# Cosine layer of a three-stage kernel: column slices in pairs, summed in one PSUM bank

## The chip, the cores and the metric

The kernel runs on one core of one Trainium2 chip. The metric is the device time of one execution in microseconds, the median of three runs. The engines are named as the profile names them: PE is TensorE (PEld its weight loads), DVE VectorE, ACT ScalarE, POOL GpSimd, SP SyncE.

## What is computed

The reference, cut to what matters here, chains an attention, a layer with a cosine in it, and a mixture of four ReLU experts over 2304 tokens of width 512:

```python
x = attn_out.transpose(0, 2, 1, 3).reshape(2304, 512)   # from 4 batches, 8 heads, 576 rows
# cosine layer: w_in 512 x 2048, w_out 2048 x 512
h = x @ w_in
g = h * np.cos(h)
x = g @ w_out
# experts: w1 4 x 512 x 1024, w2 4 x 1024 x 512
for e in range(4):
    out += p[:, e:e + 1] * (np.maximum(x @ w1[e], 0.0) @ w2[e])
```

The weights of the cosine layer come as 64-bit floats. The kernel narrows them to 32 bits itself, with integer operations.

## The kernel before

Every matrix product is done in split form: each operand is a high and a low part, and `mm3` issues three matmuls for one product.

Only the cosine layer changes. Its 2048 hidden columns are cut in 8 slices `s` of 256, its tokens in 4 batches `b` of 576. One (slice, batch) is a **unit**, and the list `order` (L410 and L411) holds 32 units, numbered `n`: first slices 0 and 1 batch by batch (n = 0 to 7), then each slice from 2 to 7 with its four batches (n = 8 to 31). A unit goes in two halves, `th` = 0 and 1, of 288 columns. For each half:

- `hidden1` (L353): 12 matmuls into `hp`, then a chain: ACT scales (`y`, L373) and rounds (`kk`, L375), DVE subtracts (L376), ACT takes the sine (L384), DVE multiplies (L385), ACT makes the high part of `gt` and POOL the low part (both L98 and L99 in `split`).
- `output1` (L389): 24 matmuls, 6 into each of four PSUM banks `op`, one for each 128 output rows `d`. DVE empties each bank: a copy for slice 0 (L404), an add into the accumulator `acc` in SBUF (L406) for the others. The output of a half is issued two halves after its hidden part (list `pend`).

Before its hidden part a unit needs `vw`, the slice's weights projected by the attention's small factor. In the later stage `project_two` (L333) does this for two units at once, 16 short matmuls each, on a 64x32 tile of the array.

A slice's weights come by `load_in` and `load_out`. Each calls `narrow` (L117) on two blocks; a block is one DMA, one ACT operation and three DVE operations (L127, L128, L131). `load_out` also splits the result (L104 on ACT, L106 shared between POOL and DVE). In `step1` the weights of slice s+1 are loaded during the four units of slice s: one block in each unit.

In time the kernel has three stages. Up to about 165 us the attention runs, eight parts of it, with the units n = 0 to 5 between them. Then, with `wide` set, hidden parts are worked in one piece of 576 columns and n = 6 to 31 follow without other work, up to about 456 us. The experts (L557 to L642) take the rest. At the seam `build_x` (L490, on DVE and ACT) prepares the experts' input, and `load2` (L523) loads and prepares their first two weight sets on the ACT queue, POOL, ACT and DVE, at marks taken from the last hidden parts. The weight sets lie in the pool `wc`, on the right side of SBUF where the attention's tiles were. A list scheduler fixes the order of instructions on each engine.

## Time and profile before

| | us |
|---|---|
| median of 3 runs | 1225.07 (1224.25 to 1225.99) |
| the profiled execution | 1226.03 |
| its span in the trace | 1223.9 |
| PE busy | 1178.7 (96% of the span) |
| DVE busy | 878.6 (72%) |
| POOL busy | 524.2 (43%) |
| ACT busy | 485.7 (40%) |

About 2.1 us of the profiled execution lie outside the span. A share of busy time is a mean over three unlike stages, so the table alone does not say what limits any one of them; the rows further down go stage by stage. A matmul's busy time overlaps its neighbour's, so for PE the distances between starts tell more than the busy time.

### The profile page before, as it was taken

Reading aid. Unit: us, or ns where it says so; the run is one execution under the profiler, and the core shown is the slowest. Engines: PE = TensorE matmul, PEld = TensorE weight load, DVE = VectorE, ACT = ScalarE, POOL = GpSimd, SP = SyncE. Lnnn points to the kernel's source line nnn. Section 1 sums busy time; section 2 is a strip of 40 time slices with the busy share of each in tenths; the row PEclk is TensorE's granted clock in tenths of the full one; section 3 lists DMA queues with packets and bytes.
Section 4 is the critical chain, followed back from the end, with each engine's and each line's share of the span. In section 5 each row is a group of like instructions: output and inputs, shape, how many; then the busy total and the mean of one; then the engine's idle time right before and its main releaser. Section 6 shows DMA issues by size and latency. Waiting matters only on the chain.

```text
span 1223.9 us, 20033 instructions
## 1 busy us (share of the span) xinstructions
PE 1178.7 (96%) x7946; PEld 1051.9 (86%) x7946; DVE 878.6 (72%) x1566; ACT 485.7 (40%) x854; POOL 524.2 (43%) x612
## 2 busy tenths in 40 slices
PE   7788999999999989999999999999999999999998
PEld 5566789999899888889899898888989889888997
DVE  5897988988888688666666666678666666666665
ACT  2475666666566663232223223244222322322221
POOL 0443533332333852445345444546544544453420
PEclk7598999999999999999999999999999999999999
DMA  9952011111112110111111111113211111111102
GB/s 223 249 155 71 21 35 53 52 39 62 39 53 70 37 51 18 35 52 53 35 52 53 35 36 54 50 36 118 63 35 42 60 38 35 53 52 36 52 1 78
DMA packets 50318, 72.88 MB, mean 60 GB/s; under 512 B 4913, under 2 KB 33585, under 8 KB 50225
## 3 DMA queue, kind: packets, MB, share of 16 engines
q1 hardware_dynamic: 43344, 55.88, 16.2%
q10 hardware_dynamic: 6880, 15.73, 4.2%
q8 instruction: 62, 1.02, 0.3%
q14 instruction: 32, 0.25, 0.1%
HBM read 66.88 MB, written 4.72 MB: 59 GB/s over the span
## 4 chain that ended last, share of the span: by engine, by line
PE 70%; DVE 16%; DMA 7%; ACT 3%; issue 2%; POOL 1%; SPq 0%; ACTq 0%; DVEq 0%; POOLq 0%
PE op L142 37%; PE hp L142 30%; DVE acc L406 3%; DVE y L376 2%; DMA raw<-in_moe_w_out_dram 2%; DMA raw<-in_moe_w_in_dram 2%; DVE y L385 2%; DVE raw L127 1%; DVE raw L128 1%; PE kvp L218 1%; DMA raw<-in_moe_w_dram 1%; DMA q<-in_q_dram 1%; DMA phi<-in_phi_dram 1%; DVE x L506 1%; DMA kv<-in_v_dram 1%
## 5 line engine op out<-in xcount | busy, mean ns | idle before, releaser
L142 PE MATMUL op<-wb,ht 128*128 128x512 f32 x1728 | 439.3, 396 | 0.0
L142 PEld LDWEIGHTS hp<-x,wa 128*128 128x128 f32 x2688 | 380.3, 189 | 24.5 <-DVE x L506 3.7
L142 PE MATMUL hp<-x,wa 128*128 128x320 f32 (+1 forms) x2688 | 393.5, 295 | 3.3 <-DVE x L506 3.0
L142 PEld LDWEIGHTS op<-wb,ht 128*128 128x128 f32 x1728 | 312.7, 188 | 58.4
L638 DVE SCALAR_TENSOR_TENSOR acc<-op,p_all,acc 128x512 f32<-128x512 f32 x270 | 201.6, 748 | 137.0 <-PE op L142 136.8
L142 PE MATMUL op<-gt,wo 128*128 128x288 f32 x1536 | 229.9, 300 | 12.3 <-DVE acc L406 5.3
L142 PEld LDWEIGHTS op<-gt,wo 128*128 128x128 f32 x1536 | 210.2, 189 | 26.8 <-DVE acc L406 7.5
L106 POOL TENSOR_TENSOR wb<-raw,wb 128x256 fp32r<-128x256 f32 x124 | 90.1, 757 | 224.4 <-ACT wb L104 224.4
L609 ACT ACTIVATE ht<-c 128x256 fp32r<-128x256 f32 (+3 forms) x128 | 71.8, 562 | 283.5 <-DVE c L579 283.5
L99 POOL TENSOR_TENSOR gt<-y,gt 128x576 fp32r<-128x576 f32 x52 | 81.1, 1559 | 159.0 <-ACT gt L98 108.7
L610 DVE SCALAR_TENSOR_TENSOR ht<-c,ht 128x256 fp32r<-128x256 f32 (+3 forms) x128 | 94.7, 740 | 63.1 <-ACT ht L609 63.1
L549 POOL TENSOR_TENSOR wa<-raw,wa 128x256 fp32r<-128x256 f32 x96 | 69.4, 749 | 148.5 <-ACT wa L539 148.5
L142 PE MATMUL hp<-attnT,vw 128*128 128x288 f32 x768 | 120.7, 304 | 7.3 <-DVE y L385 6.8
L142 PEld LDWEIGHTS hp<-attnT,vw 128*128 128x128 f32 x768 | 108.3, 192 | 14.1 <-issue 5.0
L579 DVE TENSOR_TENSOR c<-hp,u 128x256 f32<-128x256 f32 (+1 forms) x192 | 87.3, 457 | 42.3 <-PE hp L142 37.9
L549 POOL TENSOR_TENSOR wa<-tt,wa 128x256 fp32r<-128x256 f32 x128 | 110.7, 894 | 2.3 <-PE op L142 1.2
L406 DVE TENSOR_TENSOR acc<-op,acc 128x288 f32<-128x288 f32 x224 | 95.8, 448 | 9.1 <-PE op L142 9.0
L586 ACT COPY p<-hp 128x256 f32<-128x256 f32 x64 | 25.7, 401 | 112.5 <-PE hp L142 112.5
L384 ACT ACTIVATE y<-y 128x576 f32<-128x576 f32 (+1 forms) x76 | 46.1, 608 | 51.2 <-DVE y L376 42.2
L98 ACT ACTIVATE gt<-y 128x576 fp32r<-128x576 f32 (+1 forms) x76 | 46.1, 606 | 38.6 <-DVE y L385 38.5
L376 DVE SCALAR_TENSOR_TENSOR y<-kk,y 128x576 f32<-128x576 f32 x52 | 52.0, 1000 | 8.0 <-ACT kk L375 7.5
L385 DVE TENSOR_TENSOR y<-hp,y 128x576 f32<-128x576 f32 (+1 forms) x76 | 49.6, 653 | 7.6 <-ACT y L384 7.5
(101 smaller groups left out, 1035.0 us busy)
## 6 DMA issues: line engine op xcount, KB each, us to landing
raw<-in_moe_w_dram SPq DMA_DIRECT2D x60, 512.0 KB, 3.5
raw<-in_moe_w_out_dram ACTq DMA_DIRECT2D x14, 512.0 KB, 3.5
raw<-in_moe_w_in_dram ACTq DMA_DIRECT2D x12, 512.0 KB, 3.7
kv<-in_k_dram SPq DMA_DIRECT2D x16, 288.0 KB, 5.8
kv<-in_v_dram SPq DMA_DIRECT2D x16, 288.0 KB, 6.6
q<-in_q_dram SPq DMA_DIRECT2D x8, 576.0 KB, 8.2
out_dram<-acc SPq DMA_DIRECT2D x18, 256.0 KB, 2.0
phi<-in_phi_dram SPq DMA_DIRECT2D x8, 288.0 KB, 6.9
```

The lines of the kernel that those rows point to most:

```text
L98: nc.scalar.activation(out=hi, in_=src, func=ACTF.Copy)
L99: (eng or nc.vector).tensor_tensor(out=lo, in0=src, in1=f32(hi), op=ALU.subtract)
L106: (nc.vector if early and c % 512 else nc.gpsimd).tensor_tensor(out=t[:, 1, c:c + 256], in0=src[:, c:c + 256], in1=f32(t[:, 0, c:c + 256]) ...
L142: nc.tensor.matmul(out=ps, lhsT=lt(a), rhs=rt(b), start=first and i == 0, stop=last and i == 2, skip_group_check=more,)
L376: nc.vector.scalar_tensor_tensor(out=y, in0=kk, scalar=ROUND, in1=y, op0=ALU.subtract, op1=ALU.subtract)
L385: nc.vector.tensor_tensor(out=y, in0=hv, in1=y, op=ALU.mult)
L406: nc.vector.tensor_tensor(out=dst, in0=op[:, :TH], in1=dst, op=ALU.add)
L549: pool.tensor_tensor(out=wa[:, 1, o], in0=src, in1=f32(wa[:, 0, o]), op=ALU.subtract)
L579: nc.vector.tensor_tensor(out=out, in0=ps[:, :n], in1=sb, op=ALU.add)
L609: nc.scalar.activation(out=ht[:, 0, fc, lo:], in_=c[:, fc, lo:], func=ACTF.Relu)
L610: nc.vector.scalar_tensor_tensor(out=ht[:, 1, fc, lo:], in0=c[:, fc, lo:], scalar=0.0, in1=f32(ht[:, 0, fc, lo:]), op0=ALU.max, op1=ALU.su ...
L638: nc.vector.scalar_tensor_tensor(out=dst, in0=op, scalar=pe, in1=dst, op0=ALU.mult, op1=ALU.add)
```

## The change

The units of n = 2 to 7 and those of slices 3 to 6 are worked in **pairs** of slices with the same batch: hidden parts of both slices, then one output that sums the products of both slices in the same PSUM bank (12 matmuls to a bank) and empties the bank once. Slice 2 (n = 8 to 11) and slice 7 (n = 28 to 31) stay single, as do n = 0 and 1. The output of a pair goes to the queue in two entries of two banks each. `gt` gets a fourth buffer.

A pair needs the weights of two slices, so the loads move: both slices 3 and 4 are loaded during the four units of slice 2 (two blocks in a unit), slices 5 and 6 during n = 12 to 19 (one block in a unit), slice 7 during n = 20 to 23, none in n = 24 to 27. The tiles of slices 2, 5 and 6 lie in a new pool `wd` on the right side, where attention's were; `wc` opens after `wd` is closed.

```diff
-            wi[s] = cw.tile([128, KD, FS], F32, tag="wi", name="wi")
+            wi[s] = (wd[0] if s in (2, 5, 6) else cw).tile([128, KD, FS], F32, tag="wi", name="wi")
...
-        gt = cs.tile([128, 2, NFC, TH], F32R, tag="g", name="gt", bufs=3)
+        gt = cs.tile([128, 2, NFC, TH], F32R, tag="g", name="gt", bufs=4)
...
-    def output1(s, b, th, gt, wo):
-        for d in range(KD):
+    def output1(units, th, gts, ds):
+        b = units[0][1]
+        k = len(units)
+        for d in ds:
...
-            for fc in range(NFC):
-                mm3(
...
+            for j, (s, _) in enumerate(units):
+                for fc in range(NFC):
+                    mm3(
+                        op[:, :TH],
+                        lambda x: wo[s][:, x, fc, d * 128:d * 128 + 128],
+                        lambda x: gts[j][:, x, fc, :],
+                        j == 0 and fc == 0,
+                        j == k - 1 and fc == NFC - 1,
+                    )
...
-    order += [(s, b) for s in range(2, NS1) for b in range(B)]
...
+    order += [(2, b) for b in range(B)]
+    order += [(s, b) for s0 in (3, 5) for b in range(B) for s in (s0, s0 + 1)]
+    order += [(7, b) for b in range(B)]
+    assert NS1 == 8 and len(order) == NS1 * B
+    groups, n0 = [], 0
+    for n in [1, 1] + [2] * (B - 1) + [1] * B + [2] * (2 * B) + [1] * B:
+        groups.append(list(range(n0, n0 + n)))
+        n0 += n
+
+    jobs = {}
+    for j, n in enumerate((8, 9, 10, 11)):
+        for th in range(2):
+            jobs[n, th] = ((load_in, load_in, load_out, load_out)[j], (3, 4, 3, 4)[j], th)
+    for j in range(8):
+        jobs[12 + j, 0] = ((load_in, load_in, load_out, load_out)[j // 2], (5, 6, 5, 6)[j // 2], j % 2)
+    for j in range(4):
+        jobs[20 + j, 0] = ((load_in, load_out)[j // 2], 7, j % 2)
...
+    def layer1():
+        for gi, group in enumerate(groups):
+            pair = len(group) == 2
+            for th in range(2):
+                gts = []
+                for k, n in enumerate(group):
+                    if (n, th) in jobs:
+                        f, s, part = jobs[n, th]
+                        f(s, marks[-1], part)
+                    gts.append(hidden1(order[n][1], th, vws[n]))
+                    units = [order[i] for i in group]
+                    if not pair:
+                        queue.append((units, th, gts, range(KD)))
+                    elif k == 1:
+                        queue.extend((units, th, gts, ds) for ds in (range(0, 2), range(2, 4)))
+                    if len(queue) + (pair and k == 0) > 2:
+                        output1(*queue.pop(0))
+                    if (th, k) == (int(pair), 0):
+                        project_next(gi)
+                    yield
...
+    wd_ctx = ExitStack()
+    wd[0] = wd_ctx.enter_context(tc.tile_pool(name="wd", bufs=2, side="right", reuse_waits="tile"))
+    load_in(2)
+    next(steps)
+    next(steps)
+    load_out(2)
+    for _ in steps:
+        pass
+    for p in queue:
+        output1(*p)
+    wd_ctx.close()
     wc = ctx.enter_context(tc.tile_pool(name="wc", bufs=2, side="right", reuse_waits="tile"))
```

Over the whole program the adds of L406 fall from 224 to 136; the 32 copies of L404 stay, and so do all matmuls, all narrowing steps, and the operations of POOL. In the code after, L376, L385 and L406 are L377, L386 and L410, L340 is L341, and L535 to L538 and L549 are L574 to L577 and L588.

Three places show what moves. The first is PE in the middle of the wide stage, around a projection. Before (`gt` is the cosine's output, `wo` a slice's output weights, `vw_ps` the projection), the 16 matmuls of each projection stand in a row:

```order
L142 MATMUL op_3630<-gt_3487,wo_3083 128x288 x5
L142 MATMUL op_3638<-gt_3487,wo_3083 128x288 x5
L142 MATMUL op_3646<-gt_3487,wo_3083 128x288 x5
L142 MATMUL op_3654<-gt_3487,wo_3083 128x288 x6
L340 MATMUL vw_ps_3662<-wi_3222,vz_99 32x256 x8
L340 MATMUL vw_ps_3662<-wi_3222,vz_100 32x256 x8
L142 MATMUL op_3708<-gt_3542,wo_3083 128x288 x6
L142 MATMUL op_3716<-gt_3542,wo_3083 128x288 x6
L142 MATMUL op_3724<-gt_3542,wo_3083 128x288 x6
L142 MATMUL hp_3688<-attnT_98,vw_3420 128x288 x12
```

After, at the corresponding place in a pair of slices 3 and 4, on PE:

```order
L142 MATMUL op_3088<-gt_2945,wo_2475 128x288 x5
L142 MATMUL op_3148<-gt_2945,wo_2475 128x288 x6
L142 MATMUL op_3162<-gt_2945,wo_2475 128x288 x6
L341 MATMUL vw_ps_3102<-wi_2146,vz_101 32x256 x4
L142 MATMUL op_3074<-gt_3002,wo_2627 128x288
L142 MATMUL op_3088<-gt_3002,wo_2627 128x288
L341 MATMUL vw_ps_3102<-wi_2146,vz_101 32x256 x4
L341 MATMUL vw_ps_3102<-wi_2261,vz_101 32x256 x4
L142 MATMUL op_3074<-gt_3002,wo_2627 128x288 x5
L142 MATMUL op_3088<-gt_3002,wo_2627 128x288 x5
L341 MATMUL vw_ps_3102<-wi_2261,vz_101 32x256 x4
L142 MATMUL hp_3128<-attnT_96,vw_2882 128x288 x12
```

The banks op_3074 and op_3088 take products of both slices (wo_2475, wo_2627), and the projection is cut in three pieces with output matmuls between them. In the wide stage projections are interrupted 13 times in this way, once in the pair n = 6 and 7 and 12 times in the pairs n = 12 to 27; before, never.

The second place is DVE during the units of slice 2, where the output weights are narrowed (`raw64`, `wf`) and split (`wo`). Before:

```order
L127 TENSOR_SCALAR raw64_2559<-raw64_2559 128x512
L406 TENSOR_TENSOR acc_73<-op_2551,acc_73 128x288
L385 TENSOR_TENSOR y_2504<-hp_2507,y_2504 128x576
L128 SCALAR_TENSOR_TENSOR raw64_2559<-raw64_2559 128x512
L131 SCALAR_TENSOR_TENSOR wf_2442<-raw64_2559 128x512
L406 TENSOR_TENSOR acc_73<-op_2594,acc_73 128x288
L406 TENSOR_TENSOR acc_73<-op_2602,acc_73 128x288
L376 SCALAR_TENSOR_TENSOR y_2571<-kk_2572,y_2571 128x576
L406 TENSOR_TENSOR acc_73<-op_2610,acc_73 128x288
L106 TENSOR_TENSOR wo_2565<-wf_2442,wo_2565 128x256 x2
L406 TENSOR_TENSOR acc_73<-op_2618,acc_73 128x288
L385 TENSOR_TENSOR y_2571<-hp_2574,y_2571 128x576
```

After, on DVE, in the same units:

```order
L127 TENSOR_SCALAR raw64_2537<-raw64_2537 128x512
L106 TENSOR_TENSOR wo_2475<-wf_2407,wo_2475 128x256 x2
L128 SCALAR_TENSOR_TENSOR raw64_2537<-raw64_2537 128x512
L386 TENSOR_TENSOR y_2481<-hp_2484,y_2481 128x576
L410 TENSOR_TENSOR acc_73<-op_2566,acc_73 128x288
L410 TENSOR_TENSOR acc_73<-op_2574,acc_73 128x288
L131 SCALAR_TENSOR_TENSOR wf_2536<-raw64_2537 128x512
L377 SCALAR_TENSOR_TENSOR y_2543<-kk_2544,y_2543 128x576
L410 TENSOR_TENSOR acc_73<-op_2582,acc_73 128x288
L127 TENSOR_SCALAR raw64_2621<-raw64_2621 128x512
L410 TENSOR_TENSOR acc_73<-op_2590,acc_73 128x288
L128 SCALAR_TENSOR_TENSOR raw64_2621<-raw64_2621 128x512
```

There a block was narrowed in every second half; now one is narrowed in every half (raw64_2537, then raw64_2621), with as many adds between them as before.

The third place is POOL near the end of the layer, where the experts' first weights are prepared (`tt`, `wa`, `wb`) between the low parts of `gt`. Before, around the second half of n = 29 (gt_4966):

```order
L99 TENSOR_TENSOR gt_4888<-y_4886,gt_4888 128x576
L538 TENSOR_TENSOR tt_5402<-raw_5400,tt_5402 128x256
L549 TENSOR_TENSOR wa_5403<-tt_5402,wa_5403 128x256 x4
L535 TENSOR_TENSOR tt_5701<-raw_5699 128x256
L537 TENSOR_TENSOR tt_5701<-raw_5699 128x256
L99 TENSOR_TENSOR gt_4966<-y_4964,gt_4966 128x576
```

After, on POOL, around the same half (gt_4790):

```order
L99 TENSOR_TENSOR gt_4712<-y_4710,gt_4712 128x576
L588 TENSOR_TENSOR wa_5205<-tt_5204,wa_5205 128x256 x4
L588 TENSOR_TENSOR wa_5231<-raw_5228,wa_5231 128x256 x3
L574 TENSOR_TENSOR tt_5230<-raw_5228 128x256
L576 TENSOR_TENSOR tt_5230<-raw_5228 128x256
L106 TENSOR_TENSOR wb_5248<-raw_5246,wb_5248 128x256 x2
L99 TENSOR_TENSOR gt_4790<-y_4788,gt_4790 128x576
```

Between these two low parts 7 operations stood before, 11 now. The first of the experts' operations on POOL stood behind the second half of n = 26; it now stands behind the first half of n = 28.

## Rows read from the trace of the kernel before

**Rows 1.** Busy time by stretch (all engines), experts' stage: the columns, then the row.

```profile
core 0: us, PE busy (x) PEld busy (x) DVE busy (x) ACT busy (x) POOL busy (x), PEclk, DMA share, GB/s
500.00:1200.00 700.00, 700.00 (x4086) 627.33 (x4085) 446.78 (x758) 197.45 (x364) 331.46 (x431) 1.00 0.15 47
```

**Rows 2.** The same view: four units of the cosine layer, twice; then its end.

```profile
183.47:225.47 42.00, 41.42 (x353) 39.40 (x353) 37.13 (x67) 26.47 (x42) 15.59 (x11) 1.00 0.17 51
353.80:396.38 42.58, 41.41 (x354) 39.35 (x353) 36.97 (x67) 26.19 (x42) 14.64 (x11) 1.00 0.19 57
396.38:456.00 59.62, 54.37 (x436) 50.72 (x436) 45.67 (x79) 37.32 (x59) 41.24 (x43) 1.00 0.17 49
```

**Rows 3.** Timeline of PE, wide stage: start, duration, line, tiles, count, idle before.

```profile
172.91 0.66 PE L340 MATMUL vw_ps<-wi,vz 64*32 64x256 f32 x16
...
297.55 1.74 PE L142 MATMUL hp<-attnT,vw 128*128 128x288 f32 x12
...
302.86 3.35 PE L142 MATMUL op<-gt,wo 128*128 128x288 f32 x24
306.05 1.74 PE L142 MATMUL hp<-attnT,vw 128*128 128x288 f32 x12
307.63 3.34 PE L142 MATMUL op<-gt,wo 128*128 128x288 f32 x24
310.90 1.09 PE L340 MATMUL vw_ps<-wi,vz 64*32 64x256 f32 x32
311.93 2.66 PE L142 MATMUL op<-gt,wo 128*128 128x288 f32 x18
...
324.83 3.04 PE L142 MATMUL op<-gt,wo 128*128 128x288 f32 x21 [0.54 <-DVE acc L406]
```

**Rows 4.** Waits of PE, 225.47 to 396.38 us: total, times, longest.

```profile
PE op L142 <- DVE acc L406: 3.4, 8, 0.7
PE hp L142 <- DVE y L385: 0.9, 3, 0.3
```

**Rows 5.** Instructions by line and shape: busy us, mean ns, idle before.

```profile
L549 POOL TENSOR_TENSOR wa<-tt,wa 128x256 fp32r<-128x256 f32 x128 | 110.7, 894 | 2.3 <-PE op L142 1.2 <-ACT wa L543 1.2
...
L406 DVE TENSOR_TENSOR acc<-op,acc 128x288 f32<-128x288 f32 x224 | 95.8, 448 | 9.1 <-PE op L142 9.0
...
L99 POOL TENSOR_TENSOR gt<-y,gt 128x576 fp32r<-128x576 f32 x52 | 81.1, 1559 | 159.0 <-ACT gt L98 108.7 <-PE op L142 39.4 <-issue 10.8
L549 POOL TENSOR_TENSOR wa<-raw,wa 128x256 fp32r<-128x256 f32 x96 | 69.4, 749 | 148.5 <-ACT wa L539 148.5
...
L104 ACT ACTIVATE wb<-raw 128x1024 fp32r<-128x1024 f32 x32 | 33.9, 1061 | 42.5 <-PE op L142 42.3 <-DMA raw<-in_moe_w_dram 0.2
...
L128 DVE SCALAR_TENSOR_TENSOR raw<-raw 128x512 uint32<-128x512 uint32 x32 | 22.4, 700 | 0.0
...
L131 DVE SCALAR_TENSOR_TENSOR wf<-raw 128x512 uint32<-128x512 uint32 x16 | 11.9, 743 | 0.2
```

**Rows 6.** Timeline of DVE and POOL near 301 and 306 us.

```profile
300.75 1.88 POOL L99 TENSOR_TENSOR gt<-y,gt 128x576 fp32r<-128x576 f32 x1 [5.40 <-PE op L142]
...
301.62 1.62 DVE L376 SCALAR_TENSOR_TENSOR y<-kk,y 128x576 f32<-128x576 f32 x1
...
305.93 1.47 POOL L99 TENSOR_TENSOR gt<-y,gt 128x576 fp32r<-128x576 f32 x1 [3.30 <-ACT gt L98]
...
306.00 0.81 DVE L406 TENSOR_TENSOR acc<-op,acc 128x288 f32<-128x288 f32 x2
```

**Rows 7.** Busy time by stretch, as in rows 1: two stretches of the attention stage.

```profile
100.00:110.00 10.00, 10.00 (x74) 6.78 (x74) 5.11 (x10) 4.51 (x7) 3.39 (x2) 0.52 0.03 4
...
120.00:130.00 10.00, 8.81 (x99) 7.57 (x97) 9.62 (x16) 7.84 (x15) 4.86 (x4) 1.00 0.23 61
```

**Rows 8.** Timeline of PE at the end of the cosine layer.

```profile
412.49 2.91 PE L142 MATMUL op<-gt,wo 128*128 128x288 f32 x20 [0.98 <-POOL gt L99]
```

**Rows 9.** DMA issues: tiles, queue, count, size, median us to landing.

```profile
raw<-in_moe_w_dram SPq DMA_DIRECT2D x60, 512.0 KB, 3.5
```

More of the change, by code (lines that the diff above doesn't have):

```diff
@@ L408, in tile_kernel @@
     wide = [False]
-    pend = []
+    queue = []
     order = [(s, b) for b in range(B) for s in range(2)]
-    order += [(s, b) for s in range(2, NS1) for b in range(B)]
-    def project_next(n):
-        if n + 1 < len(order) and n + 1 not in vws:
-            if wide[0]:
-                project_two([i for i in (n + 1, n + 2) if i < len(order) and (i == n + 1 or order[i][0] == order[n + 1][0])])
-            else:
-                project(n + 1)
-    def step1(n):
-        s, b = order[n]
-        for th in range(2):
-            if n >= 8 and th == 0 and s + 1 < NS1:
-                (load_in, load_out)[b // 2](s + 1, marks[-1], b % 2)
-            pend.append((s, b, th, hidden1(b, th, vws[n]), wo[s]))
-            if len(pend) > 2:
-                output1(*pend.pop(0))
-            if th == 0:
-                project_next(n)
+    order += [(2, b) for b in range(B)]
@@ new lines, in tile_kernel, with project_next @@
+    for j in range(8):
+        jobs[12 + j, 0] = ((load_in, load_in, load_out, load_out)[j // 2], (5, 6, 5, 6)[j // 2], j % 2)
+    for j in range(4):
+        jobs[20 + j, 0] = ((load_in, load_out)[j // 2], 7, j % 2)
+    def project_next(gi):
+        if gi + 1 == len(groups):
+            return
+        ns = [n for n in groups[gi + 1] if n not in vws]
+        if not ns:
+            return
+        if not wide[0]:
+            for n in ns:
+                project(n)
+            return
+        if len(ns) == 1 and gi + 2 < len(groups) and len(groups[gi + 2]) == 1:
+            ns += groups[gi + 2]
+        project_two(ns)
@@ L448, in tile_kernel @@
     load_out(1, exps[1])
-    nu = 0
+    steps = layer1()
     for n in range(2, np_):
```

24 lines of the change are left out of this document (5 added, 19 removed).

## The prediction

> **What bounds the kernel now.** I read the busy time by stretch first, because the table's 96% for PE mixes three stages. In the experts' stage PE is busy for all of 700 us at full granted clock while DVE has 447 us of work [rows 1]. Nothing that the change does there can be seen in the time, so I count that stage as unchanged. All gains and losses lie before about 456 us.
>
> In the wide stage the reader should see two engines close together. The projections mark equal periods of four units. Five of them run from 183.47 to 396.38 us, 42.58 us each on average; the first and the last are shown. DVE is busy for 37 us of each, 88%, and PE for 41.4 us [rows 2]. Busy time flatters PE, so I take the distances between starts: 24 matmuls of 288 columns begin 3.19 us before the next group (302.86 to 306.05), 0.133 us each, and a projection of 32 takes 1.03 us to the next start (310.90 to 311.93) plus 0.08 us on entering (307.63 to 310.90 is 3.27) [rows 3]. Four units are 288 such matmuls and two projections: 288 x 0.133 = 38.3, plus 2 x 1.1 = 2.2, is 40.5 us. So a period loses 42.6 - 40.5 = 2.1 us. What it loses to is in the waits: PE waits for DVE to empty a bank (line L406) 3.4 us in four periods and for the multiply L385 0.9 us [rows 4]; one such stop is the 0.54 us at 324.83 [rows 3]. The named 4.3 us are the lower bound of what DVE costs PE in four periods, the whole excess of 8.3 us the upper one.
>
> **The change, part by part.** All sums stand against the profiled execution, 1226.03 us, which is 0.96 us above the median of 1225.07.
>
> *Pairs n = 12 to 27 (four periods).* An add costs DVE 0.405 us back to back (two in 0.81) [rows 6]; its mean of 448 ns contains waiting [rows 5]. A period has 16 adds fewer, 6.5 us of 37, so DVE falls to about 30.5 us in 40.5, 75%. The cover that DVE lacked is then there: the waits for banks and for L385 should nearly vanish. I take 7.5 us of the 8.3 as removed, nearer the upper end, because the first matmul after a stop also comes late and goes with it. Against that, two outputs wait for one eviction and banks are held longer; at the place printed from the order, 28 matmuls or more lie between the last use of a bank and its next, over 3.5 us at 0.133 against 0.4 for the add, so I leave 0.5 us for that and for the cosine's chain. Then the projections: 12 more pieces here. A whole projection of 16 lasts 0.66 us and one of 32 1.09, so 16 short matmuls cost 0.43 and starting and leaving a piece 0.23, with 0.08 for entering 0.31 us [rows 3]. It is on PE's own path and nothing hides it: 12 x 0.31 = 3.7 us (0 if the cuts lie in time that PE would have waited). Pairs: -7.5 + 0.5 + 3.7 = -3.3 us, from -7.8 to +0.5.
>
> *Single units n = 8 to 11.* Here the adds are as many as before, and the loads double: four more blocks with three DVE steps each, 0.70 and 0.74 us and a third (L127) taken like the first, 2.14 us in all, is 8.6, and two more pieces of L106, as large as a half of these steps, make about 1.2 [rows 5]. DVE's load in this period is 37 + 9.8 = 46.8 us against PE's 40.5, so DVE becomes the bound. If the period stretches to DVE's load at the 96% that DVE reaches in the attention stage [rows 7], it is 48.8 us, +6.2 us; if the following pairs, where DVE has 10 us to spare, take all that four PSUM banks and two hidden tiles let it owe (some 3 us by the distances above), +1.2 us. I take +4.0, between the two, since DVE's order puts most of the extra steps ahead of the multiply that PE waits for. The added DMAs are four on the ACT queue, behind the same marks; I price them at 0 since they are asked for a unit ahead of their use.
>
> For the same steps there is a rule of the Trainium skill. The trace shows a subtract of L376, with two inputs in SBUF, lasting 1.62 us beside a `gt` operation of POOL, and two adds of L406, with one input in SBUF and one in PSUM, lasting only 0.81 beside another [rows 6]. The Trainium skill, "SBUF — State Buffer", section "Who interferes with whom", says that a DVE instruction with two SBUF inputs and a GpSimd instruction that reads SBUF lock each other out for a whole instruction, and that one with at most one SBUF input does not contend. By that rule, with which these two rows agree, the adds that go were free of the lock and the steps L128, L131 and L106 that crowd into this period are not: ten such steps, POOL busy about 40% of the time (15 of 42 us before [rows 2], and its half of two more splits), half of a 1.5 us operation each, is an estimate of 3 us more here. The means of rows 5 already hold such waits, so the sum goes without it; by the rule the sum below would be about zero.
>
> *Pair n = 6, 7, and the load of slice 2.* DVE has 8 adds fewer in a stretch that PE nearly fills; one projection is cut. -0.5 + 0.3 = -0.2 us.
>
> *Attention stage, n = 2 to 5.* The order has 15 evictions fewer on DVE before the first wide multiply, 6.1 us. DVE is the fuller engine there (9.62 of 10 us, PE 8.81, from 120 to 130 us), but not everywhere: from 100 to 110 us PE runs at a granted clock of 0.52, its 1.2 GHz level, with DVE half idle [rows 7]. Of the 6.1 us I count 2.4; bounds are 0 and the 5 us that PE is idle if the 1.2 us in ten of that row hold for the some 45 us of the stage that remain. A dip that falls elsewhere could also cost: I allow +2.
>
> *End of the layer.* PE is idle for 59.6 - 54.4 = 5.2 us from 396.38 to 456 us [rows 2]. The experts' weights keep POOL busy there for 41 us, and stops such as the 0.98 us at 412.49 for POOL's `gt` are seen [rows 8]. After, that work starts about three halves later, so the idle time before about 415 us (about 2.1 us) goes. But it is denser: behind gt_4712 stand four, three, two and two operations of 0.75 to 0.89 us, about 8.9 us, then gt_4790 itself, 1.56 us [rows 5]. A half lasts about 5.1 us. The hidden part at 297.55 ended its matmuls at 299.3 and its low part on POOL at 307.4 [rows 3, 6], 8.1 us, with a subtract of 1.62 us that usually takes 0.8; so I take 7 us for this chain where DVE is less loaded. gt_4790, held behind this row, comes about 7 + 8.9 + 1.6 - 5.1 = 12.4 us behind them, and PE's order leaves 8.9 us of matmuls between: a stop of 3.5 us, in place of about 3.1 us of stops that stand there now. With about 0.8 more for what queues behind it: -2.1 + 4.3 - 3.1 = -0.9 us, from -4 to +5.
>
> Other edits: the fourth `gt` buffer and the pool `wd` issue nothing. PE's matmuls are the same.
>
> Sum: -3.3 + 4.0 - 0.2 - 2.4 - 0.9 = -2.8 us, so 1223.2 us for a profiled execution like this one and **1222.3 us** for the median.
>
> **The rivals.** A measurement of this kernel can tell about 0.2%, 2.45 us, from no change.
>
> A, the forecast: 1222.3 us, within 1220 to 1224.5. It sits on the edge between faster and the same. Chance 0.45.
>
> B, the gain is eaten on DVE during slice 2: the single period stretches by the full 6.2 us (or by the lock named above), so the sum is -2.8 + 2.2 to 3 = about -0.2, and with no gain in the attention stage +2. 1225 to 1227 us. For it speaks DVE's load of 46.8 us; against it the spare time in the pairs behind. Chance 0.20.
>
> C, slower, by POOL at the end of the layer: the weights `wb` in the row ahead of gt_4790 wait for their DMA and the ACT split, so that POOL stands still with gt_4790 behind it. That is 3.5 us to landing [rows 9] and 1.06 us on ACT [rows 5], about 4.5 us, and the next halves of `gt` push once more, about 1.5: -2.8 + 6 = +3.2 us, 1228.3 us. It decides if that DMA is issued less than 9 us before POOL reaches the split. For it: the order shows the row; against it: the DMA is issued on another queue and may be early enough. Chance 0.13.
>
> D, the larger gain: the attention stage takes 5 us off and DVE's debt of slice 2 is paid in the pairs, so that the period loses 1.2 us only: -3.3 + 1.2 - 0.2 - 5 - 0.9 = -8.2, 1216.9 us, up to 1219. For it: DVE is the fuller engine ahead of the wide stage. Chance 0.22.
>
> That the change does not do what it says can be left out: the order shows 88 adds gone.
>
> **How the numbers follow.** Faster by over 0.2% means below 1222.6 us: all of D and half of A, 0.46. Within 0.2%: most of the other half of A and most of B, 0.34. Slower: C and the rest of B, 0.20. The range takes A, B and nearly all of C and D: 1215.5 to 1229 us; the likeliest case's own is 1220 to 1224.5.
>
> **What would show it.** In the profile after, periods n = 12 to 27 should take about 41.8 us with DVE near 75% and hardly any wait of PE for the accumulator; the period of slice 2 about 46 to 47 us with DVE above 95%; the first wide projection should start about 2 us earlier; and at the end of the layer one stop of some 3 us for `gt` behind POOL should stand where several small ones stood. The experts' stage should last as long as before. If the pairs' periods stay above 42.5 us, the pieces of the projections or the chain to `gt` cost more than I think; if the period of slice 2 stays below 44, DVE's debt is carried further than I allow; if the first experts' matmul comes later than before by more than the rest explains, C holds.

## The result and the profile after

The changed kernel takes 1236.78 us (median of 4 runs, 1234.29 to 1238.57) against 1224.66 us for the kernel before (4 runs). The ratio is 1.010, with a 95% interval of 1.0072 to 1.0128: it is slower, by 12 us, outside the range of the prediction.

The span of the profiled execution went from 1223.9 to 1232.5 us. To see where the 8.6 us are, I cut both traces at the starts of the same projections on PE and at the experts' first matmul:

| stretch | before, us | after, us | difference |
|---|---|---|---|
| start to projection for n = 8 | 183.47 | 182.42 | -1.05 |
| n = 8 to 13 (to the projection for n = 14) | 64.01 | 72.45 | +8.4 |
| n = 14 to 27 (to the projection for n = 28) | 148.90 | 149.62 | +0.7 |
| end of the cosine layer (to the experts' first matmul) | 59.79 | 60.33 | +0.5 |
| from there to the end | 767.7 | 767.7 | 0 |

The busy time of the kernel after by such stretches (columns as in [rows 1]): two units each of n = 8 to 13, then four units of pairs twice, the end of the layer, and the experts:

```profile
core 0: us, PE busy (x) PEld busy (x) DVE busy (x) ACT busy (x) POOL busy (x), PEclk, DMA share, GB/s
182.42:203.74 21.32, 21.32 (x178) 19.84 (x177) 15.84 (x26) 12.11 (x21) 5.70 (x4) 1.00 0.31 89
203.74:229.34 25.60, 21.81 (x177) 19.94 (x177) 22.64 (x41) 14.61 (x24) 8.10 (x6) 1.00 0.29 91
229.34:254.87 25.53, 21.88 (x176) 19.96 (x177) 24.05 (x39) 15.30 (x24) 10.21 (x7) 1.00 0.14 43
254.87:298.02 43.15, 42.65 (x354) 39.56 (x354) 32.19 (x50) 24.76 (x41) 13.29 (x10) 1.00 0.16 49
340.31:382.61 42.30, 41.85 (x347) 38.84 (x347) 28.94 (x45) 25.12 (x40) 14.57 (x11) 1.00 0.09 26
404.49:464.82 60.33, 55.52 (x440) 51.40 (x440) 42.23 (x71) 36.86 (x58) 40.66 (x41) 1.00 0.18 54
500.00:1200.00 700.00, 700.00 (x4081) 627.36 (x4080) 446.34 (x758) 200.27 (x367) 334.89 (x435) 1.00 0.15 47
```

And of the kernel before, the two stretches of two units that answer to the second and third row (n = 10 to 13):

```profile
204.49:225.47 20.98, 20.58 (x177) 19.68 (x177) 18.58 (x34) 12.95 (x21) 7.26 (x5) 1.00 0.17 51
225.47:247.48 22.01, 21.07 (x178) 19.70 (x177) 19.64 (x35) 13.17 (x22) 7.19 (x7) 1.00 0.18 50
```

The experts' row is the same as in [rows 1]: 700 us of 700. The pairs' rows answer to [rows 2]: DVE has fallen from 37 to 32 or 29 us in four units, as it should, and yet four units take 42.3 to 43.2 us as before. In the second and third row after, DVE is busy for 22.6 and 24.1 us of 25.6 and 25.5, where it had 18.6 and 19.6 before, and two units take 25.6 us instead of 21 and 22. Together these are the units n = 10 to 13: DVE is busy for 46.7 of 51.1 us, where it was 38.2 of 43.0. PE's longest stops there, from its timeline in the kernel after (start, duration, count, idle before):

```profile
217.27 1.84 PE L142 MATMUL hp<-attnT,vw 128*128 128x288 f32 x12 [1.21 <-DVE y L386]
...
226.11 3.19 PE L142 MATMUL op<-gt,wo 128*128 128x288 f32 x22 [1.09 <-DVE acc L410]
...
232.67 3.19 PE L142 MATMUL op<-gt,wo 128*128 128x288 f32 x22 [1.76 <-POOL gt L99]
...
243.70 1.82 PE L142 MATMUL hp<-attnT,vw 128*128 128x288 f32 x12 [1.02 <-DVE y L386]
```

They are behind the multiply (L386), the bank (L410) and `gt`: stops of 1.0 to 1.8 us, where [rows 3] and [rows 4] had 0.5 to 0.7 us now and then.

### The profile page after: what moved, and what is told of

The parts are those of the page before. It is cut to its first block, busy times and chain, and to the rows that moved or that the text cites. A ratio compares the mean times of both kernels' runs of the same rounds, so it can differ in the third digit from the quotient of the medians.

```text
span 1232.5 us, 19941 instructions
## 1 busy us (share of the span) xinstructions
PE 1182.2 (96%) x7946; PEld 1052.9 (85%) x7946; DVE 848.2 (69%) x1478; ACT 488.6 (40%) x856; POOL 525.7 (43%) x612
## 3 DMA queue, kind: packets, MB, share of 16 engines
q8 instruction: 62, 1.02, 0.4%
## 4 chain that ended last, share of the span: by engine, by line
PE 71%; DVE 3%; DMA 2%; POOL 1%; ACT 1%; issue 1%; ACTq 0%; DVEq 0%; POOLq 0%
PE op L142 39%; PE hp L142 31%; DMA raw<-in_moe_w_dram 1%; PE vw_ps L341 1%; DVE y L377 1%; DVE x L545 1%; DMA raw<-in_moe_w_in_dram 1%; DMA raw<-in_moe_w_out_dram 1%; POOL wa L588 1%; DVE y L386 0%; DVE acc L410 0%; POOL gt L99 0%; DVE wo L106 0%; POOL wb L106 0%; ACT y L385 0%
## 5 line engine op out<-in xcount | busy, mean ns | idle before, releaser
L142 PE MATMUL op<-gt,wo 128*128 128x288 f32 x1536 | 233.2, 302 | 12.4 <-POOL gt L99 4.9
L588 POOL TENSOR_TENSOR wa<-raw,wa 128x256 fp32r<-128x256 f32 x96 | 70.0, 757 | 148.9 <-ACT wa L578 148.9
L618 DVE TENSOR_TENSOR c<-hp,u 128x256 f32<-128x256 f32 (+1 forms) x192 | 87.3, 458 | 42.3 <-PE hp L142 37.8
L588 POOL TENSOR_TENSOR wa<-tt,wa 128x256 fp32r<-128x256 f32 x128 | 111.5, 901 | 1.2 <-ACT wa L582 1.2
L377 DVE SCALAR_TENSOR_TENSOR y<-kk,y 128x576 f32<-128x576 f32 x52 | 56.9, 1095 | 20.8 <-ACT kk L376 20.3
L410 DVE TENSOR_TENSOR acc<-op,acc 128x288 f32<-128x288 f32 x136 | 58.8, 451 | 16.4 <-PE op L142 16.3
L385 ACT ACTIVATE y<-y 128x576 f32<-128x576 f32 (+1 forms) x76 | 46.2, 608 | 58.4 <-DVE y L377 49.4
L386 DVE TENSOR_TENSOR y<-hp,y 128x576 f32<-128x576 f32 (+1 forms) x76 | 49.8, 656 | 20.8 <-ACT y L385 19.8
```

Source lines behind the costliest of these rows:

```text
L142: nc.tensor.matmul(out=ps, lhsT=lt(a), rhs=rt(b), start=first and i == 0, stop=last and i == 2, skip_group_check=more,)
L377: nc.vector.scalar_tensor_tensor(out=y, in0=kk, scalar=ROUND, in1=y, op0=ALU.subtract, op1=ALU.subtract)
L385: nc.scalar.activation(out=y, in_=y, func=ACTF.Sin, scale=-TWO_PI if wide[0] else TWO_PI)
L386: nc.vector.tensor_tensor(out=y, in0=hv, in1=y, op=ALU.mult)
L410: nc.vector.tensor_tensor(out=dst, in0=op[:, :TH], in1=dst, op=ALU.add)
L588: pool.tensor_tensor(out=wa[:, 1, o], in0=src, in1=f32(wa[:, 0, o]), op=ALU.subtract)
```

## Experiments

The theories formed from the two traces: (1) the pieces of the cut projections cost PE what the removed adds had given back; (2) the doubled loads of slices 3 and 4 are paid on PE's path, through the first pair as well; (3) the experts' weights, late and dense, keep the end from getting shorter. The rival to all three: a pair costs PE something of its own, by banks held longer or a longer way to `gt`. All times below are medians; the stretches are from one trace each, cut as in the table above. Each ratio is to runs of the kernel before that were taken beside the kernel of its row; their medians are the first row, so medians of two rows can differ by a microsecond for that alone.

| kernel | us | ratio to before (95%) | n = 8 to 13 | n = 14 to 27 | end |
|---|---|---|---|---|---|
| before | 1223.7 to 1225.2 | | 64.0 | 148.9 | 59.8 |
| after | 1236.78 | 1.0100 (1.0072 to 1.0128) | 72.5 | 149.6 | 60.3 |
| after, once more | 1236.62 | 1.0100 (1.0067 to 1.0134) | 73.1 | 150.4 | 60.3 |
| projections whole | 1230.78 | 1.0055 (1.0037 to 1.0074) | 71.6 | 145.1 | 62.4 |
| no loads of slice 4 | 1227.05 | 1.0030 (1.0011 to 1.0049) | 64.1 | 149.4 | 60.7 |
| slice 4 fetched, not narrowed | 1229.10 | 1.0039 (1.0019 to 1.0059) | 64.4 | 149.7 | 61.3 |
| loads spread | 1235.13 | 1.0083 (1.0058 to 1.0108) | 70.0 | 150.5 | 60.7 |
| whole and spread | 1228.31 | 1.0027 (1.0014 to 1.0039) | 69.5 | 145.3 | 61.3 |
| third narrowing buffer | 1240.00 | 1.0124 (1.0095 to 1.0152) | 71.1 | 149.5 | 61.6 |
| stairs | 1217.64 | 0.9933 (0.9913 to 0.9953) | 62.5 | 146.5 | 56.3 |
| stairs, cut | 1223.54 | 0.9991 (0.9974 to 1.0008) | 64.3 | 149.1 | 57.6 |
| stairs, all single | 1222.33 | 0.9979 (0.9962 to 0.9997) | 64.6 | 150.3 | 58.2 |
| stairs, late weights | 1221.43 | 0.9970 (0.9954 to 0.9986) | 62.6 | 145.9 | 59.3 |

### The changed kernel once more

> The changed kernel once more, to see which of its stretches repeat. Theory: from the projection for n = 8 on they repeat within 0.5 us (72.5 to n = 14, 149.6 to n = 28, 60.3 to the experts), and the spread of several us between runs lies in the attention stage before it. Rival: the 72.5 us were the chance of one execution.

Measured: 73.1, 150.4 and 60.3 us. The stretches repeat within 0.8 us, a little more than expected, so the 72.5 us were no chance. The start did not tell more here (182.34 against 182.42), but see the stairs below.

### Projections whole

```diff
+                    if (th, k) == (int(pair), 0) and wide[0]:
+                        project_next(gi)
                     if len(queue) + (pair and k == 0) > 2:
                         output1(*queue.pop(0))
-                    if (th, k) == (int(pair), 0):
+                    if (th, k) == (int(pair), 0) and not wide[0]:
                         project_next(gi)
```

> The changed kernel with one edit: in the wide stage the next projection is issued ahead of the output instead of behind it, so that its 16 or 32 short matmuls stand in a row again; all else as changed. Theory 1 (cuts): in the changed kernel's trace a piece of 8 short matmuls takes 0.56 us to the next start and a whole 16 takes 0.59, so a cut costs about 0.66 us with its entries and exits; 13 cuts are 8 us of the 12 that were lost. Expected: about 1229 us, and 40.5 to 41 us for four units of the pairs instead of 42.3. Rival (pairing itself: banks held longer, or the chain to gt, which the pieces only fill): the period of the pairs stays near 42.3 us, waits of PE for gt take the place of the pieces, 1235 to 1237 us.

Measured: 1230.78 us, 6.0 less. In the pairs n = 14 to 27 it is 4.5 us, for 10 cuts that stood there: 0.45 us each. The edit also moves the projection ahead of the output, so the price of a cut alone has to come from PE's rows. The busy time of four units of pairs and of six microseconds at the layer's end:

```profile
253.65:295.31 41.66, 41.26 (x354) 39.41 (x353) 32.25 (x50) 24.86 (x41) 13.81 (x10) 1.00 0.17 51
...
436.00:442.00 6.00, 5.64 (x23) 5.67 (x24) 1.85 (x3) 2.62 (x4) 6.00 (x7) 0.50 0.10 33
```

Four units now take 41.7 us (41.5 on average over the 14): less than 42.3, not the 40.5 to 41 that I expected. How a cut costs what it does is in PE's timeline. (The program issues 8 short matmuls for a unit's projection, as the order printed ahead shows; the trace records each twice, so a unit is 16 there.) A cut projection of two units in the kernel after:

```profile
404.49 0.66 PE L341 MATMUL vw_ps<-wi,vz 64*32 64x256 f32 x14
405.07 0.53 PE L142 MATMUL op<-gt,wo 128*128 128x288 f32 x2
405.53 0.66 PE L341 MATMUL vw_ps<-wi,vz 64*32 64x256 f32 x14
406.12 1.59 PE L142 MATMUL op<-gt,wo 128*128 128x288 f32 x10
407.64 0.62 PE L341 MATMUL vw_ps<-wi,vz 64*32 64x256 f32 x4
408.19 0.40 PE L142 MATMUL op<-gt,wo 128*128 128x288 f32 x1
```

and a whole one in this kernel:

```profile
398.77 1.09 PE L341 MATMUL vw_ps<-wi,vz 64*32 64x256 f32 x32
399.79 2.27 PE L142 MATMUL op<-gt,wo 128*128 128x288 f32 x15
```

The three pieces of 14, 14 and 4 take 0.58, 0.59 and 0.55 us to the next start; the middle one holds the last 2 of the first unit and 12 of the second. A whole unit of 16 takes 0.59 (172.91 to 173.50 in the kernel before, the next row after the first of [rows 3]) and two units 1.02. So the time hardly depends on how many there are, up to a unit's 16: the program puts a unit's short matmuls on different parts of the array, the rows read as if these ran side by side, and a piece of a unit lasts as long as the whole. The Trainium skill, "TensorEngine Tiling (Array Packing)", section "Key Properties", says that different tiles can execute in parallel; the rows agree, with 0.55 us for 4 and 0.59 for 16, and add what a cut does to it. Each piece also costs PE 0.19 us on entering and leaving: the ten output matmuls from 406.12 to 407.64 take 1.52 us instead of 1.33. The two cuts of this projection thus come to 0.58 + 0.59 + 0.55 - 1.02 + 2 x 0.19 = 1.08 us, 0.54 each. A projection with a single cut, as at 254.87 us (pieces of 20 and 12, 0.98 and 0.58 us), pays 0.73 for it by the same working: the piece of 20 holds a whole unit and 4 of the next, and lasts nearly as long as two.

In this trace 2.1 us of the gain are lost again at the end, which takes 62.4 us. PE stood 2.9 us behind the multiply, and around the end of that stop its clock fell to 0.50, the 1.2 GHz level, until 442 us (last row of the busy times above); 12 matmuls took 3.2 us instead of 1.7:

```profile
436.36 3.22 PE L142 MATMUL hp<-attnT,vw 128*128 128x288 f32 x12 [2.89 <-DVE y L386]
```

### Loads of slice 4 left out

```diff
-    for j, n in enumerate((8, 9, 10, 11)):
+    for j, n in enumerate((8, 10)):
         for th in range(2):
-            jobs[n, th] = ((load_in, load_in, load_out, load_out)[j], (3, 4, 3, 4)[j], th)
+            jobs[n, th] = ((load_in, load_out)[j], 3, th)
...
+                    if (n, th) == (11, 0):
+                        wi[4], wo[4] = wi[3], wo[3]
```

> The changed kernel without the loads of slice 4: its units use slice 3's weights, so four blocks of narrowing and one split fewer on DVE, POOL, ACT and DMA in the units of slice 2 (part of the computation is left out). Theory 2 (DVE crowded there): the stretch from the projection ahead of slice 2 to that ahead of the second pair, 72.5 us in the changed kernel against 64 before, falls by 7 to 9 us, about 1228.5 us. Rival (the first pair is slow for another reason, such as the new pool or banks held longer): the stretch falls by at most 4 us, 1233 us or more.

Measured: 1227.05 us, 9.7 less, and n = 8 to 13 in 64.1 us, as before the change, with the pairs in place. The busy time of the first pair:

```profile
226.28:247.44 21.16, 20.64 (x175) 19.69 (x175) 17.70 (x32) 12.85 (x21) 6.41 (x5) 1.00 0.17 51
```

The first pair is not slow by itself: 21.2 us. The crowded loads are the whole of the 8.4 us.

### Slice 4 fetched, but not narrowed

```diff
             nc.scalar.activation(out=hif, in_=hif, func=ACTF.Copy, scale=2.0 ** -112)
+            if not dve:
+                continue
...
-            jobs[n, th] = ((load_in, load_in, load_out, load_out)[j], (3, 4, 3, 4)[j], th)
+            jobs[n, th] = ((load_in, fetch_in, load_out, fetch_out)[j], (3, 4, 3, 4)[j], th)
...
+                    if (n, th) == (11, 0):
+                        wi[4], wo[4] = wi[3], wo[3]
```

`fetch_in` and `fetch_out` call `narrow` with `dve` false, so that a block is fetched and scaled but not narrowed.

> As the run without the loads of slice 4 (its units use slice 3's weights; part of the computation is left out), but the four DMAs of slice 4 and their four ACT operations are put back; only DVE's narrowing steps for it, and the split, stay out. Theory (DVE's work is what crowds n = 8 to 13): the stretch from the projection for n = 8 to that for n = 14 stays at 64 to 65.5 us. Rival (the DMAs, their buffers and the ACT queue are the crowd): 68 us or more of the changed kernel's 72.5.

Measured: 64.4 us for n = 8 to 13, and 1229.1 us. With four DMAs and four ACT operations back the stretch stays short; the first pair:

```profile
232.25:253.41 21.16, 20.64 (x175) 19.70 (x175) 17.50 (x32) 13.59 (x22) 6.39 (x5) 1.00 0.18 55
```

So it is the narrowing on DVE together with the split, which was left out too (half of its pieces are POOL's, and it has one operation of ACT), not the transfers. What the split's part is, no run shows.

### Loads spread, alone and with whole projections

```diff
-    for j, n in enumerate((8, 9, 10, 11)):
-        for th in range(2):
-            jobs[n, th] = ((load_in, load_in, load_out, load_out)[j], (3, 4, 3, 4)[j], th)
+    for n, th, f, s, part in (
+        (7, 0, load_in, 3, 0), (6, 1, load_in, 3, 1), (8, 0, load_in, 4, 0), (8, 1, load_in, 4, 1),
+        (9, 0, load_out, 3, 0), (10, 0, load_out, 3, 1), (11, 0, load_out, 4, 0), (11, 1, load_out, 4, 1),
+    ):
+        jobs[n, th] = (f, s, part)
```

> The changed kernel with the loads of slices 3 and 4 spread from n = 6 to 11 instead of 8 to 11, nothing left out, projections cut as in the changed kernel. Theory 2: DVE's debt of about 9 us in that stretch is spread over 50% more units, and 4 to 6 us come back: 1231 to 1233 us. Rival (the amount of loading counts, not its crowding): no gain, 1236 us, since the same blocks then delay n = 6 and 7.

> Both edits: projections whole and loads spread. If theories 1 and 2 hold and are separate, the gains add: 8 and 5 us, about 1224 us, near the kernel before (1224.7). If pairing itself is what costs, it stays above 1231 us.

Measured: 1235.13 us, 1.6 less than the kernel after, within what its runs scatter, and 1228.31 us with both edits, 2.5 less than with whole projections alone and short of the 1224 expected. The first expectation was a miss: n = 8 to 13 takes 70.0 us, 2.4 less and not 4 to 6. But its rival does not hold either: n = 6 and 7 take 21.9 us from the projection ahead of them to that for n = 8 (163.67 to 185.59), and 22.4 in the kernel after (160.03 to 182.42). The projection for n = 8 does start 3.2 us later, but all of that lies ahead of these units, in the attention stage, where the granted clock (third number from the end) differs. From 120 to 140 us, the kernel after and then the loads spread:

```profile
120.00:140.00 20.00, 17.34 (x180) 14.10 (x179) 13.37 (x30) 15.79 (x28) 8.12 (x8) 0.91 0.12 31
```

```profile
120.00:140.00 20.00, 16.73 (x142) 12.24 (x141) 11.42 (x26) 11.60 (x21) 6.17 (x8) 0.66 0.11 31
```

Spreading over six units takes back 2 to 3 us of the 8.4; the larger part of the debt stays.

### A third buffer for the narrowing

```diff
-            raw = cw.tile([128, c, 2 * m], U32, tag="raw64", name="raw64")
+            raw = cw.tile([128, c, 2 * m], U32, tag="raw64", name="raw64", bufs=3)
```

> The changed kernel with a third buffer for the blocks that are narrowed (raw64), nothing else. In its trace DVE stands 2.1 us behind a block's DMA at 216 us, with the multiply that PE waits for queued behind it, and a block's DMA can only be issued when the block two before it is done. Theory a (the late DMA is a good part of what the crowded loads cost): 2 to 3 us less in the stretch of 72.5 us, 1234 us. Theory b (DVE's amount of work, 46.8 us against 40.5, decides): within 1 us of 72.5, 1236 to 1237 us.

Measured: 1240.0 us; n = 8 to 13 in 71.1 us, 1.3 less, and the projection for n = 8 starts 3.4 us later, as soft a number as above. DVE still waits for blocks, 2.7 us in three stops where it was 3.5 in two. The 1.3 us are soft too, for the stretch holds a dip of the clock to 0.50: the 12 matmuls behind the stop of 2.67 us take 2.93 us to the next start instead of some 1.6:

```profile
246.06 3.09 PE L142 MATMUL hp<-attnT,vw 128*128 128x288 f32 x12 [2.67 <-DVE y L386]
248.99 3.23 PE L142 MATMUL op<-gt,wo 128*128 128x288 f32 x23
```

Without the dip the stretch would be some 2.6 us shorter than after, as theory a has it, but the median is 3 us longer. Inconclusive between the two.

### The stairs

The experiments say what a better order needs: pairs, whole projections, one slice loaded in every four units, and the experts' pool free early. Pairs that overlap like stairs give all four:

```diff
-    order += [(2, b) for b in range(B)]
-    order += [(s, b) for s0 in (3, 5) for b in range(B) for s in (s0, s0 + 1)]
-    order += [(7, b) for b in range(B)]
+    order += [(2, 2), (2, 3)]
+    order += [(s, b) for s0 in range(2, 7) for b in ((0, 1) if s0 % 2 == 0 else (2, 3)) for s in (s0, s0 + 1)]
+    order += [(7, 2), (7, 3)]
...
-    for n in [1, 1] + [2] * (B - 1) + [1] * B + [2] * (2 * B) + [1] * B:
+    for n in [1, 1] + [2] * (B - 1) + [1] * 2 + [2] * 10 + [1] * 2:
...
+    jobs[6, 1] = (load_in, 3, 0)
+    jobs[8, 0] = (load_in, 3, 1)
+    jobs[8, 1] = (load_out, 3, 0)
+    jobs[9, 1] = (load_out, 3, 1)
+    for s, n in ((4, 10), (5, 14), (6, 18), (7, 22)):
+        for th in range(2):
+            jobs[n, th] = (load_in, s, th)
+            jobs[n + 2, th] = (load_out, s, th)
```

The pool `wc` opens first, and `wd` with one buffer (slices 2 and 5) below it; the projection stands ahead of the output.

> A new order, nothing left out: pairs overlap like stairs. Slice 2 single for batches 2 and 3, then pairs (2,3) for batches 0 and 1, (3,4) for 2 and 3, (4,5) for 0 and 1, (5,6) for 2 and 3, (6,7) for 0 and 1, slice 7 single for 2 and 3. So 20 of 24 later units are paired and yet one slice is loaded in every four units, as before the change. Projections stay whole; slices 2 and 5 share one buffer that lies beside the experts' pool, so that the experts' first weights can come as early as before. Theory (cuts, crowded loads and the late experts' weights were the three costs): units n = 8 to 29 take 20.3 to 20.8 us in every two, the layer's end 36 us, about 1216 us, 8 under the kernel before. Rival (a pair costs PE something of its own): no faster than before, 1224 us or more.

Measured: 1217.64 us, 0.9933 of the kernel before (0.9913 to 0.9953): faster than both kernels, by 7 us over the one before. The trace is of the slowest of its six runs, 1222.29 us. Busy time, four units each and then the end:

```profile
186.99:228.27 41.28, 40.52 (x348) 38.76 (x348) 34.98 (x60) 24.95 (x41) 14.20 (x11) 1.00 0.22 65
228.27:270.82 42.55, 42.10 (x358) 40.11 (x357) 32.98 (x52) 26.57 (x42) 14.21 (x11) 1.00 0.16 51
...
354.70:396.00 41.30, 40.92 (x350) 38.90 (x349) 29.18 (x45) 24.64 (x39) 14.98 (x11) 1.00 0.12 37
396.00:452.33 56.33, 54.50 (x441) 51.32 (x441) 39.86 (x63) 37.29 (x60) 40.53 (x41) 1.00 0.16 50
```

Four units take 41.3 to 42.6 us with DVE at 29 to 35. I expected 40.6 to 41.6. Some stops are left, behind the multiply and `gt` (waits of PE, 180 to 455 us: total, times, longest):

```profile
PE hp L142 <- DVE y L386: 3.5, 6, 1.8
PE op L142 <- POOL gt L99: 2.1, 5, 1.3
```

### The stairs with every unit single

```diff
-    for n in [1, 1] + [2] * (B - 1) + [1] * 2 + [2] * 10 + [1] * 2:
+    for n in [1, 1] + [2] * (B - 1) + [1] * 24:
```

> The stairs' order, loads, buffers and whole projections, but with every unit from n = 8 on given out alone, so all adds of the accumulator stand. What it differs by from the stairs is the pairing alone: 80 adds of 0.405 us on DVE. Theory (the pairing removes the stops of PE at 88% of DVE load, some 1.9 us in four units): 6 to 10 us slower than the stairs, about the time of the kernel before. Rival (the order and the loads make the difference, not the sums): within 2 us of the stairs.

Measured: 1222.33 us, 4.7 slower than the stairs; in the traces 273.0 against 265.3 us from the projection for n = 8 to the experts, 7.6 us. Two of its stretches, four units each:

```profile
265.95:310.76 44.81, 41.88 (x353) 39.49 (x352) 37.76 (x66) 26.03 (x42) 13.67 (x11) 1.00 0.16 48
310.76:354.05 43.29, 41.43 (x353) 39.44 (x352) 37.97 (x66) 26.09 (x42) 13.80 (x11) 1.00 0.16 50
```

and its waits over the same time as those of the stairs:

```profile
PE op L142 <- DVE acc L410: 6.0, 7, 1.2
PE hp L142 <- DVE y L386: 4.9, 8, 1.0
```

With DVE back at 37 to 38 us the waits for the bank return, 6.0 us of them, and vanish in the stairs. So the sums in one bank do what they should; the order with its whole projections and free pool gives 2 us by itself, its interval just clear of none. The medians give 4.7 us and the traces 7.6; which is nearer the worth of the pairing is not settled, as the trace of the stairs stands 4.7 us above their median.

### The stairs, cut

The projection is issued behind the output again, as in the changed kernel.

> The stairs with the projection issued behind the output again, so that 16 cuts stand inside projections of a unit, where PE waits for little else. Theory of the traces: a unit's 8 short matmuls of the program run side by side on parts of the array, each part of a cut unit takes as long as the whole, so a cut costs 0.66 us: 10.6 us over the stairs with whole projections. By the prediction's own price of 0.31 us: 5 us.

Measured: 1223.54 us, 5.9 more than the stairs, and 5.7 more in the traces from the projection for n = 8 on. That is 0.36 us for each of 16 cuts, about the price of the prediction and not the 0.66 of my later reading of the trace. A stretch of four units:

```profile
224.22:266.95 42.73, 42.73 (x354) 39.67 (x354) 31.92 (x51) 26.76 (x43) 15.10 (x11) 1.00 0.16 51
```

and the waits of PE over the same time as those of the stairs:

```profile
PE op L142 <- POOL gt L99: 2.4, 4, 1.2
PE hp L142 <- DVE y L386: 0.8, 1, 0.8
```

PE now has no idle time that the records show, 42.73 of 42.73 us, yet it is no faster than the kernel before. By the rows of the pieces a cut costs PE 0.54 to 0.73 us, of which 0.36 is seen. Part of the difference is that cuts fill time in which PE would otherwise wait: its waits fall from 5.6 us in the stairs to 3.2. The rest of it is not accounted for. A cut hides in PE's busy time, where no view of waits shows it.

### The stairs with late weights for the experts

```diff
-        w[s] = load2(s, nc.scalar, (marks[4 * s - 10], marks[4 * s - 8]))
+        w[s] = load2(s, nc.scalar, (marks[4 * s - 7], marks[4 * s - 5]))
```

> The stairs with one edit: the experts' first two weight sets are tied to marks three halves later, about where the change put them; the operations are the same. Theory (late weights crowd POOL between the last low parts of gt, and PE stops there): the end of the layer, 56.3 us from the projection for n = 28 in the stairs, grows by 3 to 5 us, 1221 us. Rival (POOL has room and only the total counts): within 1.5 us, 1218 us.

Measured: 1221.43 us, 3.8 more, and 59.3 us for the end instead of 56.3. The stops lie where POOL is full, and the clock falls behind them (busy time from 436 to 442 us):

```profile
436.00:442.00 6.00, 5.11 (x24) 4.66 (x24) 3.81 (x7) 2.90 (x6) 6.00 (x7) 0.72 0.56 175
```

PE's waits from 390 to 452 us, the two largest that lie in the layer:

```profile
PE op L142 <- DVE acc L410: 2.4, 4, 0.8
PE op L142 <- POOL gt L99: 0.5, 1, 0.5
```

So lateness costs some 3 us. Since nothing else differs from the stairs, this is shown for the stairs; for the changed kernel, which has the same weights at about that place, it is only likely. The way it takes is not the one that I expected: only 0.5 us of the waits is for `gt` on POOL, 2.4 us are for DVE's adds, and six microseconds at a clock of 0.72 are worth about 1.7 us at full clock (an estimate, 6 x 0.28). How a full POOL holds up DVE's adds there, no run shows.

The stairs and this kernel have the same instructions ahead of the projection for n = 8, and it starts at 187.0 us in the one and at 182.0 in the other. The clock in the attention stage differs, from 120 to 140 us: the stairs, then this kernel:

```profile
120.00:140.00 20.00, 16.60 (x141) 12.23 (x140) 11.70 (x26) 11.52 (x22) 6.12 (x7) 0.66 0.10 31
```

```profile
120.00:140.00 20.00, 17.15 (x173) 14.04 (x173) 13.88 (x33) 15.46 (x29) 7.54 (x8) 0.91 0.11 31
```

20 us at 0.66 instead of 0.91 are worth 5.0 us at full clock (an estimate), as much as the starts differ by. A single trace therefore cannot tell a few microseconds in that stage.

## Why the prediction was wrong

**What bounds the kernel.** Right: the experts' stage did not change, and PE and DVE are close in the wide stage. In the single-unit stairs the waits for the bank come back with DVE's load.

**Pairs n = 12 to 27, -3.3 us.** Both terms failed in size. Of the stops in a period I took 7.5 us of 8.3 as removed over 16 units, 6.6 in the 14 units of n = 14 to 27. The kernel with whole projections gained 148.9 - 145.1 = 3.8 us there. The named waits alone, my lower bound, would have been the better reading: 4.3 us in 16 units by [rows 4], 3.8 in 14. Much of what I took for stops is in PE's busy time: with whole projections four units still take 41.5 us and not my 40.5, and PE is busy for 143.8 of the 145.1 us. The cuts were priced at 0.31 us and cost 0.45 there (4.5 us for 10), or 0.54 to 0.73 on PE by their own rows. I had read the time of a piece as proportional to its matmuls, from the two whole lengths of [rows 3]; it is nearly the same for 4 as for 16. So the two terms cancel, +0.7 us measured, and four units take 42.7 us on average: above the 42.5 that I had named as the sign of costlier pieces. That pairing in itself holds little back was right: the first pair takes 21.2 us without the crowded loads, so banks held longer cannot be what made it 25.5.

**Single units, +4.0 us.** That crowded loads on DVE stop PE was right, and the size was half of what it was. The four units of slice 2 took 46.9 us instead of 42.0, +4.9, close to the +4.0. That is partly luck: DVE was busy for only 38.5 us of these 46.9, 82% and not above 95%. The load that I had put there came two units later, in n = 10 to 13, 46.7 of 51.1 us. So the step that failed is the next: I let the pairs behind, where DVE has room on average, take the rest. They did not; the first pair took 25.5 us instead of 22.0, and 21.2 with the narrowing and split of slice 4 left out, since these weights are still being narrowed there and stand ahead of the multiply that PE waits for. Together +8.4. DVE's steps were also longer than their means. The last narrowing step of the output weights in the kernel after, from 183 to 254 us (busy, mean ns):

```profile
L131 DVE SCALAR_TENSOR_TENSOR wf<-raw 128x512 uint32<-128x512 uint32 x4 | 5.0, 1252 | 0.0
```

and in the kernel before, in the same stretch of time:

```profile
L131 DVE SCALAR_TENSOR_TENSOR wf<-raw 128x512 uint32<-128x512 uint32 x2 | 1.4, 686 | 0.0
```

The single instructions show why. On DVE in the kernel after:

```profile
216.03 0.43 DVE L127 TENSOR_SCALAR raw<-raw 128x512 uint32<-128x512 uint32 x1 [2.06 <-DMA raw<-in_moe_w_out_dram]
...
223.67 2.02 DVE L377 SCALAR_TENSOR_TENSOR y<-kk,y 128x576 f32<-128x576 f32 x1
...
235.41 1.94 DVE L131 SCALAR_TENSOR_TENSOR wf<-raw 128x512 uint32<-128x512 uint32 x1
```

and on POOL:

```profile
223.64 1.43 POOL L99 TENSOR_TENSOR gt<-y,gt 128x576 fp32r<-128x576 f32 x1 [4.24 <-issue]
...
230.05 2.56 POOL L99 TENSOR_TENSOR gt<-y,gt 128x576 fp32r<-128x576 f32 x1 [3.07 <-ACT gt L98]
235.39 1.42 POOL L99 TENSOR_TENSOR gt<-y,gt 128x576 fp32r<-128x576 f32 x1 [2.77 <-issue]
```

The subtract at 223.67 and the narrowing step at 235.41 begin 0.03 and 0.02 us behind a `gt` operation of POOL and last 2.02 and 1.94 us, 0.5 to 0.6 past its end; alone they last 0.7 to 0.8. The Trainium skill, "SBUF — State Buffer", section "Who interferes with whom", says that a DVE instruction with two SBUF inputs contends with a GpSimd instruction that reads SBUF, and the trace agrees in these two pairs of rows. POOL is held as well: its `gt` operation at 230.05, beside DVE's steps, lasted 2.56 us instead of 1.4, and PE's longest stop, 1.76 us before 232.67, ends 0.06 us behind it. I left the lock's 3 us out of the sum as held in the means. It belonged in it: added to the 4.0 it would have come to 7 of the 8.4 us. An estimate from the two traces bears out the size: against the median of such instructions with none of POOL beside them, DVE's in n = 8 to 13 last 7.0 us longer in all before and 10.1 after. That all of these 3.1 us come out in PE's time is not shown; no run takes the lock away by itself. The first row of DVE also shows 2.1 us of waiting for a block's DMA, which I had priced at nothing; the third buffer did not settle its share.

**Pair n = 6, 7 and the attention stage, -2.6 us.** 1.05 us earlier in the first trace. From 90 to 130 us the granted clock was 0.91 in it and 0.87 in the kernel before, which alone is worth up to 1.6 us, so this trace shows no gain of the evictions. Beyond that it is not shown either way, for the start scatters by 5 us with the clock.

**End of the layer, -0.9 us.** +0.5. The stop behind the crowded POOL came, 1.8 us long behind one of 0.7 for the bank where I had 3.5, and the early stops went; three of 0.7 to 0.9 us stand between 437 and 443 us in their place. PE's idle time in this stretch fell by 0.4 us only, and the two cuts at 404.49, which I had counted with the pairs, add 1.1. PE in the kernel after:

```profile
452.67 0.40 PE L142 MATMUL op<-gt,wo 128*128 128x288 f32 x1 [0.67 <-DVE acc L410]
454.84 10.14 PE L142 MATMUL op<-gt,wo 128*128 128x288 f32 x69 [1.77 <-POOL gt L99]
```

With whole projections the same end costs more: 62.4 us, with a dip of the clock that I had not counted.

**The rivals.** B named the right place (DVE in the units of slice 2, with the lock) but gave it 2 to 3 us over the forecast and stopped at 1227. C's place, the end, was a small part. None had several terms fail on the same side, which is what happened. Against the prediction's steps the trace has +0.9 us in the units of slice 2 (4.9 for 4.0), +7.5 in the pairs n = 12 to 27 (3.5 in the first and 0.7 in the rest, for -3.3), +1.4 at the end and +1.6 at the start. The range was too narrow for four soft terms added up. The medians differ by 12.1 us where the spans differ by 8.6: the profiled execution of before was above its median, that of after 2.5 us below. The other 3.5 us stand in no trace. The parts that the runs took out come near the 12.1: the crowded loads 9.7 us and the cuts 6.0 by the medians, less the 3.8 that the sums in one bank gave, are 11.9.

## What to carry to other kernels

Do not count on an engine's spare time behind a crowded stretch to pay for the crowd: here the debt came due where it arose, ahead of a step that PE waited for, so spread the load to the rate at which it is used up (here by overlapping pairs) before counting a saving elsewhere. When a change lets a scheduler put work between small matmuls that share the array, price each piece as a whole group, and look at the order, for the cost hides in a busy PE, where PE's idle time does not show it. Where two engines contend on an instruction, price the added instructions at their contended duration, not at the mean.
